# Splitting the ring's loads by partition between two issuing engines

## The chip, the cores and the metric

The kernel runs on one core of a Trainium2 chip. The metric is the device time of one execution in microseconds (us). The kernel before takes 869.49 us, the median of three runs (869.4 to 870.17). One execution of it was profiled; that one took 869.43 us, of which the profile's span covers 867.6 us.

The engines are named as in the profile: PE is the matrix engine, PEld its weight loads, DVE the vector engine, ACT the scalar engine (ScalarE), POOL GpSimd and SP the sync engine (SyncE). SP does nothing here but issue transfers. Each engine works through its own instructions in the order in which they were written; an instruction that waits holds up everything behind it on that engine.

## The reference

The kernel computes two layers of a decoder for one token of 8 sequences, all in float32. Each layer is an attention block with a cache of keys and values, and a dense block with GELU. Both layers use the same weights and the same caches:

```python
def _A_ref(x, k_cache, v_cache, wq, wo):          # x 8x1x1024, caches 8x4x4096x128
    q = (x @ wq).reshape(B, Sq, Hq, Dh)           # 32 query heads, 4 heads of keys
    scores = einsum("bhqd,bhkd->bhqk", q, k) * (Dh ** -0.5)
    p = softmax(scores)
    o = einsum("bhqk,bhkd->bhqd", p, v)
    return o.reshape(B, Sq, Hq * Dh) @ wo
def _B_ref(x, w1, b1, w2, b2):                    # 1024 -> 3584 -> 1024
    h = gelu(einsum("bsd,df->bsf", x, w1) + b1)
    return einsum("bsf,fd->bsd", h, w2) + b2
x = x + _A_ref(_layernorm(x), ...)
x = x + _B_ref(_layernorm(x), ...)
x = x + _A_ref(_layernorm(x), ...)
x = x + _B_ref(_layernorm(x), ...)
```

## The kernel before, in words

Nearly all of its time goes into reading weights and caches from device memory: with 8 rows of activations each loaded element is used for little arithmetic. All loads go into one large tile of on-chip memory, `arena`, 128 partitions by 218 units of 256 floats (1 KB per partition and unit). Three areas of 64 units, A, Bb and C, take loads of 8 MB (128 partitions of 64 KB each): one sequence's keys or values for all four heads, or half of `wq` or `wo`. A fourth area is the **ring**: four slots R[0] to R[3] of 8 units, which take loads of 1 MB (128 partitions of 8 KB each).

The order of the loads is a list, `stream`, that is written out at build time: for layer 0 `wq`, then keys and values of sequences 0 to 7, then through the ring `wo` ("o0", 16 loads), `w1` ("i0", 14 loads), `w2` ("p0", 13 loads of 1 MB and two of 0.5 MB) and `wq` again ("q1", 14 loads of 1 MB, one of 0.75 MB and one of 0.5 MB). After that layer 1 goes through the caches from the last sequence to the first, in large loads again, and its `wo`, `w1` and `w2` come in large loads too. While the ring runs, the areas A, Bb and C still hold caches of the last sequences, which layer 1 uses without loading them again.

`take` marks units as used and `give` as free. `give` is called behind the matmuls that read a load last, and it calls `pump`, which issues every load at the head of `stream` whose units are free (L183 to L191). Everything is recorded in the order of the program; the issuing instruction then waits on the chip until those matmuls are done. In the kernel before, all loads of `stream` are issued by SP (L190), so SP's order is the order of `stream`.

In the ring, `expand` (L200, matmuls at L217) and `project` (L307, matmuls at L314) read one load after another; each load takes PE some eight or sixteen matmuls, then its slot is given back and the load four places further on is issued into it. Between them stand the layer norms (`layernorm`, L146: a Square at L167 and a Sqrt at L174 on ACT) and the GELU (`hidden_unit`, L280: a Tanh at L291 on ACT between DVE operations).

Of the kernel before, what the change touches and what calls it, by code (L numbers as in the profile page):

```python
# [14 lines left out]
P = 128  # L15
# [37 lines left out]
def decode_layers(ctx: ExitStack, tc: tile.TileContext, x, kc, vc, wq, wo, w1, w2, w2_low, out):  # L53


    nc = tc.nc
# [12 lines left out]
    def is_free(at, n):  # L69
        return not any(u in used for u in range(at, at + n))  # L70

    def take(at, n, who):
        assert is_free(at, n), (who, at, n)
        used.update(dict.fromkeys(range(at, at + n), who))

    def give(at, n):
        for u in range(at, at + n):
            used.pop(u)
        pump()
# [99 lines left out]

    stream = []  # L180
    held = {}

    def pump():  # L183
        while stream and is_free(stream[0][1], stream[0][2]):
            key, at, n, src = stream.pop(0)
            take(at, n, key)
            dst = arena[:, at * KB:at * KB + src.shape[1]]
            if key[0] == "low":
                dst = arena[key[1]:LOW:4, AT_LOW * KB:AT_LOW * KB + src.shape[1]]
            nc.sync.dma_start(out=dst, in_=src)  # L190
            held[key] = at, n  # L191

    def loads(name):
# [403 lines left out]
    open_queries()  # L597
    rsum = row_sums()
    pump()
    nc.vector.tensor_reduce(rsum, x_row, AX.X, ALU.add)  # L600

# [162 lines left out]
```

## Time and profile before

| | |
|---|---|
| median of 3 runs | 869.49 us |
| the profiled execution | 869.43 us, its span 867.6 us |
| PE busy / DVE busy / ACT busy | 541.9 / 175.3 / 52.9 us |
| moved from device memory | 368.47 MB, 425 GB/s over the span |
| stretch with 8 MB loads, 60 to 340 us | 432 GB/s |
| stretch of the ring, 345 to 505 us | 419 GB/s |
| stretch with large loads, 565 to 830 us | 432 GB/s |

The profile's page gives busy time per engine, then the span in 40 slices of 21.7 us each. The line DMA there is the mean busy share of the core's 16 DMA engines, in tenths; GB/s is what they moved. A DMA queue holds the transfers of one issuing engine; each transfer is cut into packets over the 16 DMA engines. The chain of waits follows the work that ended last back to the start, at each step to what released it. The answers on stretches of time give, for each stretch, its length, the busy time and count of PE, PEld, DVE, ACT and POOL, then the granted clock of PE, the busy share of the DMA engines (1.00 is all of them, all the time) and GB/s.

### The profile page before, as it was taken

The page shows a single profiled execution, that of the slowest core. Times are in us where ns is not written, and L with a number is a line of the kernel's source. Part 1 is how long each engine was busy: PE and PEld are TensorE (multiplying, and loading weights), DVE is VectorE, ACT ScalarE, POOL GpSimd, SP SyncE. Part 2 cuts the span into 40 slices and gives each one's busy share as a digit, 9 for nine tenths or more (in the row PEclk, how much of TensorE's full clock was granted, in tenths as well). Part 3 has the DMA queues.
Part 4 walks back from the last instruction along what each step waited for, and adds up shares of the span by engine and source line. Part 5 has one row for each costly group of instructions (what it writes and reads, how often), then busy time and mean ns, then how long its engine had stood idle before and what let it go on. Part 6 is the DMA issues. An engine that isn't in the chain of part 4 may idle for free.

```text
span 867.6 us, 8713 instructions
## 1 busy us (share of the span) xinstructions
PE 541.9 (62%) x3896; PEld 173.1 (20%) x3896; DVE 175.3 (20%) x458; ACT 52.9 (6%) x84; POOL 3.5 (0%) x14
## 2 busy tenths in 40 slices
PE   0556575655656566867676587776574654665677
PEld 0112121211212122221221132222121211211222
DVE  0001231313122232200110023332231313120011
ACT  0200000000000011000000010000000000000100
POOL 0000000000000000000000000000000000000000
PEclk9977787777777877766876888977787777777789
DMA  9999999999999999999999999999999999999997
GB/s 393 436 436 433 435 430 433 435 433 433 435 430 433 435 417 426 407 419 421 420 420 420 421 420 437 438 433 433 435 433 433 435 433 435 433 432 433 420 425 308
DMA packets 16669, 369.06 MB, mean 425 GB/s; under 512 B 1868, under 2 KB 2028, under 8 KB 2924
## 3 DMA queue, kind: packets, MB, share of 16 engines
q1 hardware_dynamic: 16488, 368.36, 99.3%
q8 instruction: 30, 0.49, 0.2%
q10 hardware_dynamic: 144, 0.15, 0.0%
q14 instruction: 7, 0.06, 0.0%
HBM read 368.47 MB, written 0.03 MB: 425 GB/s over the span
## 4 chain that ended last, share of the span: by engine, by line
DMA 77%; PE 20%; DVE 1%; ACT 1%; issue 0%; SPq 0%; POOL 0%; ACTq 0%; POOLq 0%
DMA arena<-in_A_k_cache_dram 22%; DMA arena<-in_A_v_cache_dram 21%; DMA arena<-in_B_w_dram 16%; DMA arena<-in_A_wo_dram 10%; DMA arena<-in_A_wq_dram 8%; PE sps L483 6%; PE sps L426 6%; PE sps L217 2%; PE sps L314 2%; PE sps L497 1%; PE spot L339 1%; PE sps L461 0%; ACT arena L450 0%; DVE arena L434 0%; ACT arena L464 0%
## 5 line engine op out<-in xcount | busy, mean ns | idle before, releaser
L426 PE MATMUL sps<-arena 128*32 128x512 f32 x992 | 142.4, 712 | 116.6 <-DMA arena<-in_A_k_cache_dram 104.4
L483 PE MATMUL sps<-arena 128*32 128x512 f32 x1024 | 151.7, 732 | 19.6 <-DMA arena<-in_A_v_cache_dram 19.6
L217 PE MATMUL sps<-arena,xnT 128*32 128x512 f32 (+3 forms) x592 | 77.0, 650 | 37.3 <-DMA arena<-in_A_wq_dram 19.3
L426 PEld LDWEIGHTS sps<-arena 128*32 128x32 f32 x992 | 31.2, 124 | 192.6 <-DMA arena<-in_A_k_cache_dram 96.8
L314 PE MATMUL sps<-arena,oT 128*32 128x256 f32 x496 | 50.5, 546 | 22.4 <-DMA arena<-in_B_w_dram 10.6
L490 DVE TENSOR_TENSOR sps<-sps,misc 128x512 f32<-128x512 f32 x64 | 44.3, 692 | 65.0 <-PE sps L483 65.0
L461 PE MATMUL sps<-ident,arena 128*128 128x128 f32 x128 | 28.8, 365 | 43.5 <-ACT arena L450 31.6
L483 PEld LDWEIGHTS sps<-arena 128*32 128x32 f32 x1024 | 33.0, 130 | 95.6 <-issue 72.5
L450 ACT ACTIVATE arena<-arena,bias 128x1024 f32<-128x1024 f32 x16 | 18.4, 1147 | 492.2 <-DVE scratch L447 492.2
L434 DVE TENSOR_SCALAR_CACHE_REDUCE arena<-sps 128x512 f32<-128x512 f32 x32 | 22.1, 691 | 124.6 <-PE sps L426 124.6
L491 DVE TENSOR_REDUCE scratch<-sps 128x128 f32<-128x512 f32 x64 | 44.2, 691 | 2.2
L499 DVE TENSOR_TENSOR oT<-sps,scratch 128x8 f32<-128x8 f32 x64 | 11.0, 172 | 160.5 <-PE sps L497 160.5
L217 PEld LDWEIGHTS sps<-arena,xnT 128*32 128x32 f32 x592 | 18.1, 127 | 84.3 <-DMA arena<-in_A_wq_dram 30.3
L497 PEld LDWEIGHTS sps<-misc,scratch 128*128 128x128 f32 x128 | 21.5, 211 | 66.0 <-DVE scratch L491 39.9
L339 PE MATMUL spot<-arena,oT 128*32 128x512 f32 x120 | 16.9, 717 | 18.9 <-DMA arena<-in_A_wo_dram 18.9
L461 PEld LDWEIGHTS sps<-ident,arena 128*128 128x128 f32 x128 | 18.2, 179 | 51.8 <-ACT arena L450 35.5
L497 PE MATMUL sps<-misc,scratch 128*128 128x8 f32 x128 | 27.4, 286 | 1.2 <-DVE scratch L491 1.2
L314 PEld LDWEIGHTS sps<-arena,oT 128*32 128x32 f32 x496 | 17.1, 142 | 53.3 <-DMA arena<-in_A_wo_dram 19.6
L339 PE MATMUL spot<-arena 128*32 128x512 f32 (+2 forms) x108 | 17.9, 682 | 1.8 <-DMA arena<-in_B_w_dram 1.8
L466 DVE COPY arena<-sps 128x512 f32<-128x512 f32 x16 | 11.1, 691 | 37.1 <-PE sps L461 37.1
L156 PE MATMUL sps<-nmean,rsum 128*128 128x64 f32 x8 | 2.0, 336 | 25.3 <-DVE rsum L600 23.7
L468 PE MATMUL sps<-scratch,misc 128*128 128x32 f32 x32 | 10.0, 404 | 12.5 <-DVE arena L466 12.5
(105 smaller groups left out, 163.2 us busy)
## 6 DMA issues: line engine op xcount, KB each, us to landing
arena<-in_B_w_dram SPq DMA_DIRECT2D x27, 1024.0 KB, 8.0
arena<-in_A_wo_dram SPq DMA_DIRECT2D x16, 1024.0 KB, 8.7
arena<-in_A_wq_dram SPq DMA_DIRECT2D x14, 1024.0 KB, 8.7
arena<-in_A_k_cache_dram SPq DMA_DIRECT2D x3, 4096.0 KB, 17.8
arena<-in_A_v_cache_dram SPq DMA_DIRECT2D x3, 4096.0 KB
arena<-in_A_v_cache_dram SPq DMA_DIRECT2D x4, 2048.0 KB, 11.2
arena<-in_B_w_dram SPq DMA_DIRECT2D x1, 6144.0 KB, 45.9
arena<-in_B_w_dram SPq DMA_DIRECT2D x1, 5120.0 KB, 39.4
```

Of the source, the lines that this page charges most:

```text
L217: nc.tensor.matmul(acc[32 * j:32 * j + 32, r * P:(r + len(ts)) * P], xnT[:, kt * B:kt * B + 32], blocks[:, ts[0] - t0:ts[-1] - t0 + 1:4], ...
L314: nc.tensor.matmul(y[32 * j:32 * j + 32, a:a + n], weights, data, start=(j not in begun), stop=stop)
L339: nc.tensor.matmul(y2[32 * j:32 * j + 32, h * CH:(h + 1) * CH], weights, data, start=((h, j) not in begun2), stop=stop)
L426: nc.tensor.matmul(ps[32 * g:32 * g + 32, :], q[:, c:c + 32], kt[:, g * CH:(g + 1) * CH], start=(j == 0), stop=(j == HKV - 1))
L434: nc.vector.tensor_scalar(row[:, half * CH:(half + 1) * CH], ps, SCALE, None, op0=ALU.mult, op1=ALU.max, accum_out=st["mx"][:, half:half + 1])
L450: nc.scalar.activation(row, row, AF.Exp, bias=bias, scale=1.0, accum_out=ls)
L461: nc.tensor.transpose(pp[:, t * P:(t + 1) * P], row[:, c:c + P], ident)
L466: nc.vector.tensor_copy(s[:, half], src)
L483: nc.tensor.matmul(o[32 * g:32 * g + 32, :], s[:, g], v[:, g * CH:(g + 1) * CH], start=(half == 0), stop=(half == NH - 1))
L490: nc.vector.tensor_tensor(blocks, blocks, sel_t.unsqueeze(2).to_broadcast([P, T, DH]), ALU.mult)
L491: nc.vector.tensor_reduce(r, o.rearrange("p (t d) -> p d t", t=T), AX.X, ALU.add)
L497: nc.tensor.matmul(po[:, 0:REP], scratch[:, a:a + DH], sel_h, start=True, stop=True)
```

## The change

Each load of "o0", "i0", "p0" and "q1" that covers at least 6 units (0.75 or 1 MB) is made as two loads. SP issues partitions 0 to 63, ACT issues partitions 64 to 127. That concerns 58 loads (16 + 14 + 13 + 15). The three loads of 0.5 MB in the ring, all large loads and everything on the compute engines stay as they are. The matmuls that read such a load wait for both halves.

```diff
+    HALVED_LOADS = ('o0', ('i0', 0), ('i0', 1), 'p0', ('q1', 0), ('q1', 1))
 
     def pump():
         while stream and is_free(stream[0][1], stream[0][2]):
...
-            nc.sync.dma_start(out=dst, in_=src)
+            if key[0] in HALVED_LOADS and n >= 6:
+                nc.sync.dma_start(out=dst[0:P // 2], in_=src[0:P // 2])
+                nc.scalar.dma_start(out=dst[P // 2:P], in_=src[P // 2:P])
+            else:
+                nc.sync.dma_start(out=dst, in_=src)
             held[key] = at, n
```

In the changed kernel the two new issuing lines are L192 (SP) and L193 (ACT), the old one is L195, and the lines behind them move down by 5.

On SP nothing moves; the rows of the ring's loads are half as high. This is SP's list from the last loads of layer 0's values to the first of layer 1's, in the kernel before:

```order
L190 DMA arena<-in_A_v_cache_dram 128x2048 x2
L190 DMA arena<-in_A_wo_dram 128x2048 x16
L190 DMA arena<-in_B_w_dram 128x2048 x27
L190 DMA arena<-in_B_w_dram 128x1024 x2
L190 DMA arena<-in_A_wq_dram 128x2048 x11
L190 DMA arena<-in_A_wq_dram 128x1536
L190 DMA arena<-in_A_wq_dram 128x2048 x3
L190 DMA arena<-in_A_wq_dram 128x1024
L190 DMA arena<-in_A_v_cache_dram 128x4096 x2
```

and with the change (`B_w` is `w1` and then `w2`):

```order
L195 DMA arena<-in_A_v_cache_dram 128x2048 x2
L192 DMA arena<-in_A_wo_dram 64x2048 x16
L192 DMA arena<-in_B_w_dram 64x2048 x27
L195 DMA arena<-in_B_w_dram 128x1024 x2
L192 DMA arena<-in_A_wq_dram 64x2048 x11
L192 DMA arena<-in_A_wq_dram 64x1536
L192 DMA arena<-in_A_wq_dram 64x2048 x3
L195 DMA arena<-in_A_wq_dram 128x1024
L195 DMA arena<-in_A_v_cache_dram 128x4096 x2
```

The places and the order are the same; 58 rows have 64 partitions in place of 128.

On ACT, which issued only the load of `x` before, the other halves now stand between its own instructions. This is the piece of the difference on ACT over layer 0's second layer norm (Square L167, Sqrt L174) and its two GELUs (Tanh, L296):

```order
+L193 DMA arena<-in_A_wo_dram 64x2048 x13
+L193 DMA arena<-in_B_w_dram 64x2048 x4
+L167 ACTIVATE scratch,ss<-x_all,nmu 128x256
+L193 DMA arena<-in_B_w_dram 64x2048 x2
+L174 ACT_TABLE_LOAD
+L174 ACTIVATE sd<-sps,misc 128x1
+L193 DMA arena<-in_B_w_dram 64x2048 x7
+L296 ACT_TABLE_LOAD
+L296 ACTIVATE scratch<-scratch 128x128
+L193 DMA arena<-in_B_w_dram 64x2048 x7
+L296 ACTIVATE scratch<-scratch 128x96
+L193 DMA arena<-in_B_w_dram 64x2048 x7
```

A half that stands behind a Square, a Sqrt or a Tanh is issued only after it, and those three stand behind the halves ahead of them, each of which waits until the matmuls have left its slot.

## The prediction

> **What bounds the kernel now.** I read the page's slices first, then its chain of waits:
>
> ```profile
> DMA  9999999999999999999999999999999999999997
> GB/s 393 436 436 433 435 430 433 435 433 433 435 430 433 435 417 426 407 419 421 420 420 420 421 420 437 438 433 433 435 433 433 435 433 435 433 432 433 420 425 308
> ...
> DMA 77%; PE 20%; DVE 1%; ACT 1%; issue 0%; SPq 0%; POOL 0%; ACTq 0%; POOLq 0%
> ```
>
> The DMA engines are busy in every slice and carry 77% of the chain: the kernel takes as long as its bytes take. But the rate is not the same throughout. From slice 15 to slice 24, where the ring runs, it is about 420 GB/s, elsewhere 433 to 436. The stretches say it more sharply (third column from the right: granted clock; then DMA share, GB/s):
>
> ```profile
> 60.00:340.00 280.00, 170.90 (x1094) 53.03 (x1094) 67.69 (x168) 13.79 (x22) 0.00 (x0) 0.77 1.00 432
> 345.00:505.00 160.00, 112.50 (x961) 35.24 (x965) 17.31 (x50) 8.95 (x15) 0.16 (x1) 0.73 1.01 419
> ```
>
> Both have a DMA share of 1.00 or 1.01: in the ring too, no DMA engine is idle. So the ring is not short of transfers in flight; its bytes only cost more engine time each. The DMA view of the same two stretches says why (queue 1 is SP's; packets, MB, share of 16 engines):
>
> ```profile
> q1 hardware_dynamic: 2421, 120.78, 99.9%
> ...
> q1 hardware_dynamic: 9251, 66.88, 101.0%
> ```
>
> Take the engine time as so much per MB and so much per packet. Stretch one: 280 us x 16 x 0.999 = 4476 engine-us for 120.78 MB and 2421 packets. Stretch two: 160 x 16 x 1.010 = 2586 for 66.88 MB and 9251 packets. The two equations give 36.8 engine-us per MB (435 GB/s over 16 engines) and 0.0136 us per packet. The ring's rate is lower because its rows are 8 KB, not 64 KB, and each is a packet. The change keeps the rows at 8 KB.
>
> How much lies ahead of a load when it is issued:
>
> ```profile
> arena<-in_B_w_dram SPq DMA_DIRECT2D x27, 1024.0 KB, 8.0
> ...
> 403.73 8.77 DMA arena<-in_B_w_dram
> 412.50 0.04 issue
> 412.55 1.11 PE sps L217 x8
> 413.67 8.77 DMA arena<-in_B_w_dram
> ```
>
> In the chain, a slot goes round in 413.67 - 403.73 = 9.94 us, during which four loads land, so one load takes 2.49 us. From issue to landing a load needs 8.0 us at the median, of which 8.0 - 2.5 = 5.5 us are spent behind earlier loads. That is the cover: a transfer issued 1 us later lands no later, while the queues are not dry.
>
> **The change part by part.** *Bytes and rows*: the same, nothing.
>
> *Completions*: each load's packets include one small one per DMA engine, which reports it done. 58 loads more, 16 engines each, are 928 packets; at 0.0136 us over 16 engines this is 928 x 0.0136 / 16 = **+0.8 us**. It lies on the DMA engines, which set the end, so all of it counts. Bounds: nothing, if the second queue's data fills the gap; 1.6 us at double price.
>
> *Two queues in place of one*: the ring's two halves now alternate on every DMA engine. The trace has one case, the load of `x` on ACT's queue beside the first 8 MB load on SP's:
>
> ```profile
> x_all<-in_A_x_dram ACTq DMA_DIRECT2D x1, 146.0 KB, 22.4
> ```
>
> 146 KB should take under half a microsecond at 435 GB/s; it takes 22.4 us because its few rows per engine wait their turn between rows of 64 KB. In just that time, slice 1 of the page, the rate is 393 of 436, a loss of 21.7 x (1 - 393/436) = 2.1 us, which includes the start of everything. So taking turns between the queues costs next to nothing there. But that load covers all 128 partitions, as nearly all others do. The nearest loads with fewer are the four of 3 partitions each near the end, and their data is too little to give a rate. What happens when each queue aims at one half of the partitions, the trace does not show. From below, I bound it by what a perfect overlap of the packets' gaps could give: the 58 loads hold 57.75 x 1.0486 = 60.6 MB, 144.5 us at 419 GB/s and 140.2 us at 432, so **-4.3 us**. From above, by the halves taking turns entirely, each at half the rate, 216 GB/s: 280.4 us, **+136 us**. I take 0 for the forecast, being nearest to the one row with two queues, and keep both ends.
>
> [...]
>
> *Issuing*: SP's transfers and those that are not full height stand in one view of line 190:
>
> ```profile
> L190 SPq DMA_DIRECT2D arena<-in_A_wo_dram x18: 327/328/431, 326.2 to 748.9; - x18
> L190 SPq DMA_DIRECT2D arena<-in_low_dram x4: 642/664/837, 786.3 to 789.0; - x4
> ```
>
> A full load takes SP 0.33 us to issue, one of 3 partitions 0.64 to 0.84 us. A half lies between them in height; I take 0.33 to 0.84 us, so at most 0.5 us later than now. On SP as on ACT there is one per 2.49 us, and 0.5 us is a tenth of the cover of 5.5 us: **0 us**. Without cover, 58 x 0.5 = 29 us.
>
> *What waits on ACT*: the halves there stand behind a Square, a table load with Sqrt, or a table load with Tanh, and hold those up in turn. ACT has room, 8.95 us busy of the ring's 160. The tightest place is the GELU:
>
> ```profile
> 422.13 1.28 ACT L291 ACT_TABLE_LOAD   x1 [19.99 <-DVE scratch L290]
> 423.43 0.31 ACT L291 ACTIVATE scratch<-scratch 128x128 f32<-128x128 f32 x1
> ...
> 422.48 1.07 PE L217 MATMUL sps<-arena,xnT 128*32 128x128 f32 x16 [0.21 <-DMA arena<-in_B_w_dram]
> ```
>
> The next half behind this Tanh becomes free when PE leaves that load, at 422.48 + 1.07 = 423.55; Tanh ends at 423.74. The half is 0.2 us late, covered. The Sqrt of the layer norm waits in turn for a half ahead of it, whose slot PE leaves one load later than now, so its table load of 1.28 us falls up to 2.5 us later. Behind it DVE takes the reciprocal, which is first used at the end of the unit, eight loads on: covered too. Price without cover: about 1.5 us at each of the four places, 6 us.
>
> *Late halves at the turns*: the program has eight counters for landed transfers, in turn. Before, eight loads could be under way; now it is eight halves, four loads, which is just the ring. At the first loads of i0 and q1 the turn is out of step and SP's half waits until ACT's half of two loads earlier has landed. Six loads are concerned. Then one load, 2.49 us, is still ahead of it, against 0.33 to 0.84 us of issue and the way to the memory. I take 0.1 us for each, **+0.6 us**, between 0 and, if each loses half a load's time, 7 us.
>
> Sum: 0.8 + 0.6 = +1.4 us on the profiled execution's 869.43 (span 867.6 and 1.8 around it): **870.9 us**, 0.06 us more when set against the median of 869.49. The end of the ring doesn't swallow it: behind it DMA stays busy (slices 24 and 25 above), so what comes late there ends late.
>
> **The rivals.** *The halves hinder each other.* If the DMA engines that carry a half together can only reach part of the write side at a time, each row takes longer, and each 1% on the row adds 1.45 us, since the ring has no slack. For it: a half covers half the partitions, and in a full load each engine's rows may go to partitions of its own. Against it: alternating rows give both halves work at every moment. It would take anything from 2% more, 872 us, past a row a third longer, 918 us, to taking turns, 869.5 + 136 = 1005 us. It decides from a row that is 2% longer than now.
>
> *The gaps close.* If two queues let one half's next row be fetched during the other's gap, the ring runs at the 432 GB/s of large rows and saves 4.3 us: 865.2 us. For it: the fitted 0.0136 us per packet. Against it: the share of 101.0% says that packets already overlap a little.
>
> *The cover fails.* ACT and SP issue different halves at different times and a load counts only when the later one is there. If issue at 0.84 us, the waits on ACT and the counters together exceed the 5.5 us, each load loses up to 0.5 us: 29 us, 898 us. Against it: the rows of ACT above.
>
> **How the numbers follow.** About 0.2%, 1.7 us, is what a measurement of this kernel can tell from no change. Forecast, no hindrance: 0.42, its own range 869 to 873; of this 0.27 lies within 0.2% and 0.15 above. Hindrance: 0.33, spread evenly from 872 to 1005. Closed gaps: 0.17. Failed cover: 0.08. So faster 0.17, same 0.27, slower 0.15 + 0.33 + 0.08 = 0.56. The range leaves out the upper part of the hindrance, beyond 955 (0.33 x 50/133 = 0.12), and the last of the closed gaps below 866 (0.05): 866 to 955 us.
>
> **What would show it.** In the changed profile, the stretch of the ring should still show a DMA share of 1.00 and close to 419 GB/s, with as many bytes on ACT's queue as on SP's, about 30 MB each. A share near 1.00 at a much lower rate, with time from issue to landing well above 8 us, would be hindrance. A share clearly below 1.00 would be failed cover, with SP or ACT named as releaser. About 430 GB/s would be closed gaps. The stretches of large loads must not change; if they do, my account of the ring is wrong.

## The result and the profile after

With the change the kernel takes 970.51 us, the median of four runs (967.6 to 979.51), against 869.44 us before: 1.118 times as long, 95% interval 1.114 to 1.121, 101 us more. The forecast was 870.9 us and the range 866 to 955; both missed. That both say slower is no merit of the forecast: its +1.4 us came from other terms, and the loss is one that it put at 0 and kept as a rival, halves that hinder each other. Where two runs of one kernel lie more than 1.5% apart, as below with 951.6 and 999.2 us, only the faster one is compared.

The page's slices of the changed kernel (a slice is 24.4 us now), its queues (queue 1 SP's, queue 10 ACT's: packets, MB, share of 16 engines), and the stretches with 8 MB loads, of the ring, and with large loads again (last columns: granted clock, DMA share, GB/s):

```profile
DMA  9999999999999999999999999999999999999997
GB/s 392 446 413 467 425 427 432 427 430 442 430 430 426 380 311 211 252 245 227 259 265 267 249 249 247 428 429 449 430 432 427 430 437 438 438 427 432 426 422 308
...
q1 hardware_dynamic: 12776, 338.08, 86.8%
q10 hardware_dynamic: 4784, 30.43, 12.7%
...
60.00:340.00 280.00, 170.20 (x1081) 52.88 (x1085) 66.86 (x164) 13.79 (x22) 0.00 (x0) 0.77 1.00 427
345.00:605.00 260.00, 132.14 (x918) 41.03 (x921) 16.27 (x50) 9.54 (x17) 0.16 (x1) 0.55 1.01 250
680.00:940.00 260.00, 156.13 (x1019) 47.55 (x1009) 56.31 (x140) 13.38 (x22) 1.17 (x1) 0.77 1.00 431
```

The large loads run as before: from 60 to 310 us at 433 GB/s against 434, and the 427 in place of 432 up to 340 us comes from the end, where ACT's first half is already loading. The ring runs at 250 GB/s in place of 419. The profiled execution is the slowest of the four, and its span is 977.6 - 867.6 = 110 us longer than that of the kernel before. The 60.6 MB of halved loads take 60.6 / 0.250 = 242 us in place of 144.5, 98 of these 110 us; with the other loads of the stretch, 65.0 MB in all, it is 260 us in place of 155, 105 of the 110. The DMA share is still 1.01: no DMA engine is idle, the same rows only take longer. The bytes are the same, 368.5 MB in all.

The chain of waits in the ring, and the page's issues of the halves:

```profile
397.91 14.63 DMA arena<-in_A_wo_dram
412.55 0.04 issue
412.59 1.98 PE sps L319 x16
414.59 14.78 DMA arena<-in_A_wo_dram
...
arena<-in_B_w_dram ACTq DMA_DIRECT2D x27, 512.0 KB, 12.4
arena<-in_A_wo_dram SPq DMA_DIRECT2D x16, 512.0 KB, 12.4
```

A slot goes round in 414.59 - 397.91 = 16.7 us where it took 9.9, and the halves shown take 12.4 us from issue to landing where a whole load took 8.0 to 8.7.

### The profile page after: what moved, and what is told of

Same layout as the page of the kernel before. It is cut to its first block, busy times and chain, and to the rows that moved or that the text cites. A ratio compares the mean times of both kernels' runs of the same rounds, so it can differ in the third digit from the quotient of the medians.

```text
span 977.6 us, 8889 instructions
## 1 busy us (share of the span) xinstructions
PE 570.5 (58%) x3896; PEld 180.4 (18%) x3896; DVE 175.6 (18%) x458; ACT 52.9 (5%) x84; POOL 3.5 (0%) x14
## 2 busy tenths in 40 slices
DMA packets 17598, 369.07 MB, mean 378 GB/s; under 512 B 2796, under 2 KB 2956, under 8 KB 3852
## 4 chain that ended last, share of the span: by engine, by line
DMA 81%; PE 17%; DVE 1%; ACT 1%; issue 0%; SPq 0%; ACTq 0%
DMA arena<-in_A_v_cache_dram 24%; DMA arena<-in_A_k_cache_dram 19%; DMA arena<-in_B_w_dram 17%; DMA arena<-in_A_wo_dram 10%; DMA arena<-in_A_wq_dram 10%; PE sps L488 5%; PE sps L431 5%; PE sps L222 2%; PE sps L319 2%; PE spot L344 1%; PE sps L502 1%; PE sps L466 0%; DVE arena L439 0%; ACT arena L455 0%; DVE scratch L496 0%
## 5 line engine op out<-in xcount | busy, mean ns | idle before, releaser
L431 PE MATMUL sps<-arena 128*32 128x512 f32 x992 | 145.2, 724 | 119.4 <-DMA arena<-in_A_k_cache_dram 107.3
L488 PE MATMUL sps<-arena 128*32 128x512 f32 x1024 | 154.4, 743 | 29.1 <-DMA arena<-in_A_v_cache_dram 29.1
L222 PE MATMUL sps<-arena,xnT 128*32 128x512 f32 (+3 forms) x592 | 88.5, 731 | 67.1 <-DMA arena<-in_B_w_dram 37.2
L319 PE MATMUL sps<-arena,oT 128*32 128x256 f32 x496 | 56.5, 600 | 63.3 <-DMA arena<-in_A_wo_dram 31.4
L319 PEld LDWEIGHTS sps<-arena,oT 128*32 128x32 f32 x496 | 19.8, 152 | 98.0 <-issue 69.1
L344 PE MATMUL spot<-arena,oT 128*32 128x512 f32 x120 | 17.9, 756 | 17.6 <-DMA arena<-in_A_wo_dram 17.6
L247 DVE TENSOR_SCALAR scratch<-sps,rs 128x512 f32<-128x512 f32 (+1 forms) x8 | 5.7, 718 | 83.8 <-PE sps L222 83.8
## 6 DMA issues: line engine op xcount, KB each, us to landing
arena<-in_B_w_dram ACTq DMA_DIRECT2D x27, 512.0 KB, 12.4
arena<-in_A_wo_dram SPq DMA_DIRECT2D x16, 512.0 KB, 12.4
```

The source lines that it names most:

```text
L222: nc.tensor.matmul(acc[32 * j:32 * j + 32, r * P:(r + len(ts)) * P], xnT[:, kt * B:kt * B + 32], blocks[:, ts[0] - t0:ts[-1] - t0 + 1:4], ...
L319: nc.tensor.matmul(y[32 * j:32 * j + 32, a:a + n], weights, data, start=(j not in begun), stop=stop)
L344: nc.tensor.matmul(y2[32 * j:32 * j + 32, h * CH:(h + 1) * CH], weights, data, start=((h, j) not in begun2), stop=stop)
L431: nc.tensor.matmul(ps[32 * g:32 * g + 32, :], q[:, c:c + 32], kt[:, g * CH:(g + 1) * CH], start=(j == 0), stop=(j == HKV - 1))
L488: nc.tensor.matmul(o[32 * g:32 * g + 32, :], s[:, g], v[:, g * CH:(g + 1) * CH], start=(half == 0), stop=(half == NH - 1))
```

## The experiments

Five theories were set against each other. A: which partitions a load covers decides how fast its rows land. B: two queues taking turns cost the time. C: a load of 64 rows is slow by itself. D and E, later, are about why two halves together don't make up for it: D, that pairs of DMA engines work on the same half at the same moment; E, that the loss comes with every such half, whatever the engines' turns. All kernels differ from the changed one only in the lines that issue the halves. The kernel before took 869.6 to 870.2 us as the median beside each set of runs.

### Both halves from one queue

```diff
-                nc.scalar.dma_start(out=dst[P // 2:P], in_=src[P // 2:P])
+                nc.sync.dma_start(out=dst[P // 2:P], in_=src[P // 2:P])
```

> Both halves of each of the 58 loads issued by SyncE, one behind the other; ScalarE issues none. Theory A (the DMA engines that carry one half share their way into the half's partitions, whatever queue it came from): as slow as the change or slower, ring at 217 to 250 GB/s, 960 to 1005 us. Theory B (two queues taking turns row by row is what costs): back to about 871 us, ring at 415 to 419 GB/s. Theory C (a row of a load of 64 partitions is slower by itself, for instance by the way its packets are made): about 970 us as the change.

The run that is compared took 951.6 us, 82 us more than before; a second took 999.2 us. The stretch of the ring in the faster one:

```profile
345.00:580.00 235.00, 130.09 (x922) 41.53 (x921) 16.93 (x50) 8.95 (x15) 0.16 (x1) 0.55 1.02 278
```

Slow with one queue too. 278 GB/s is above the 217 to 250 that A had expected, and 951.6 us below its 960, so the size was missed; but it is far from B's 415 to 419 GB/s. The second queue is not what makes the change slow; B falls. A and C stand.

### Split by columns

```diff
+                half = src.shape[1] // 2
+                nc.sync.dma_start(out=dst[:, 0:half], in_=src[:, 0:half])
+                nc.scalar.dma_start(out=dst[:, half:], in_=src[:, half:])
```

> The 58 loads split by columns in place of partitions: each half covers all 128 partitions with rows of 4 KB, one from SyncE, one from ScalarE. Theories A and C: no hindrance, but 58 x (128 + 16) more packets at 0.0136 us over 16 engines, +7 us: about 877 us, ring near 400 GB/s. Theory B: two queues take turns as in the change, over still more rows: 970 us or more.

876.89 us (ratio 1.008, 1.006 to 1.010), 7.3 us more, where 7 were worked out from the packets. The ring:

```profile
345.00:510.00 165.00, 114.77 (x965) 34.45 (x965) 17.39 (x50) 10.42 (x18) 0.16 (x1) 0.73 1.02 403
```

Two loads per slot from two engines, the same bytes, twice the packets, and next to no hindrance. What hurts is how the change cuts the load, not that it is cut. (The agreement on the microsecond is partly luck: a pair of runs further down shows that a second queue has a price of its own, which was not in the 7 us.)

### Even and odd partitions

```diff
+                nc.sync.dma_start(out=dst[0:P:2], in_=src[0:P:2])
+                nc.scalar.dma_start(out=dst[1:P:2], in_=src[1:P:2])
```

> The halves of the change, but SyncE takes the even partitions and ScalarE the odd ones, so each half spans the whole height of the memory. If the change is slow because 64 neighbouring partitions are only one half of the memory's height (A in its simplest form): hindrance gone, about 871 us, ring near 415 GB/s. If it is slow because the rows are dealt out in order over the 16 engines, so that pairs of engines meet at the same place in any half (A as pairs): slow again, 230 to 260 GB/s, 950 to 990 us. Theory C: about 970 us. Theory B: about 970 us.

884.98 us (two runs, 885.0 and 884.95), neither 871 nor 970. The stretches, and the wait that stands out, show two things at once:

```profile
356.00:360.00 4.00, 1.11 (x4) 0.71 (x4) 0.28 (x1) 1.62 (x3) 0.00 (x0) 0.50 0.04 14
368.00:372.00 4.00, 2.59 (x24) 1.01 (x20) 2.81 (x6) 0.59 (x1) 0.00 (x0) 1.00 0.09 12
376.00:520.00 144.00, 91.25 (x871) 30.68 (x864) 11.29 (x39) 8.36 (x14) 0.84 (x2) 0.77 1.01 412
...
ACT arena L469 <- DMA arena<-in_A_wo_dram: 15.7, 1, 15.7
```

From 376 us on, the ring runs at 412 GB/s: halves of 64 rows, two queues, no hindrance. C falls, since these rows are as many and as long as in the change. Before that the DMA engines stand almost idle in two gaps: at the end of the attention an ACT copy into `arena` (L469, L464 in the kernel before) waits 15.7 us for the ring's first load. No other kernel's trace has this wait; in the kernel before, the same copy waits 1.3 us for PE. A likely reason, not tested by itself, is that the rows of the strided half are taken to overlap the copy's target. So the run was made again without that.

### The same, with the ring's first four loads whole

```diff
+                if key in [('o0', i) for i in range(4)]:
+                    nc.sync.dma_start(out=dst, in_=src)
+                else:
+                    nc.sync.dma_start(out=dst[0:P:2], in_=src[0:P:2])
+                    nc.scalar.dma_start(out=dst[1:P:2], in_=src[1:P:2])
```

> Even partitions from SyncE and odd ones from ScalarE, as in the run before, but the ring's first four loads whole, so that no instruction at the end of the attention waits for a half. If the 15 us of that run over the kernel before are the stall at its first load and not the halves: 870 to 873 us, ring at 412 to 419 GB/s. If the halves cost it: about 884 us.

876.2 us (ratio 1.008, 1.006 to 1.009). The stall was 8.8 of the 15 us; 6.5 us remain, a miss of 3 us against the expected 870 to 873. The ring has 405 GB/s at a DMA share of 1.00, below the expected 412 to 419 too:

```profile
345.00:510.00 165.00, 111.31 (x993) 38.07 (x993) 17.51 (x52) 8.95 (x15) 0.84 (x2) 0.74 1.00 405
```

### One half alone: the lower, the middle, the even

Here the disputed cost stands alone: the ring's first four loads whole, then only one half of each load, all from SP. The other half is left out, so the matmuls read old data there. These are the lines of three kernels, one each:

```diff
+                    nc.sync.dma_start(out=dst[0:P // 2], in_=src[0:P // 2])   # the lower
+                    nc.sync.dma_start(out=dst[32:96], in_=src[32:96])         # the middle
+                    nc.sync.dma_start(out=dst[0:P:2], in_=src[0:P:2])         # the even
```

> The disputed cost by itself: the ring's first four loads whole, of the other 54 only partitions 0 to 63, all from SyncE; the upper halves are not loaded at all, so the ring moves about half its bytes and the matmuls read old data there. Theory A (64 neighbouring partitions from 0 on are reached over half of the write side): a half takes almost as long as a whole load did, ring at about 217 to 250 GB/s with a DMA share near 1.00, 54 x 0.524 MB at 217 GB/s = 130 us where 134 us stood before: about 865 us, 850 at 250 GB/s. Rival (both halves in flight together is what hinders): rows as fast as before, the ring limited by the matmuls, DMA share well below 1.00, 800 to 840 us.

> As the run with the lower half only, but with partitions 32 to 95 in its place: 64 neighbours too, the same bytes, the same issuing. [...] If any 64 neighbours, or any load of 64 rows, is slow: the same time as the lower half, 850 to 865 us.

> As the run with the lower half only, but with the 64 even partitions: the same bytes and rows. Theory A (the whole height is reached): rows as fast as in a whole load, ring limited by the matmuls, DMA share well below 1.00, 800 to 840 us, as with the middle half. If a load of 64 rows is slow by its packets: 850 to 865 us as the lower half.

The lower half: 875.1 us (874.4 and 875.8). The middle half: 832.4 us (831.2 and 833.5). The even half: 829.4 us (826.6 and 832.1). The last two lie in the 800 to 840 us that theory A gave for both. The ring of each, in this order:

```profile
385.00:505.00 120.00, 79.35 (x687) 24.79 (x687) 9.22 (x35) 7.97 (x14) 0.16 (x1) 0.74 1.01 209
```

```profile
385.00:465.00 80.00, 58.62 (x651) 20.96 (x647) 10.38 (x36) 8.36 (x14) 0.42 (x2) 0.90 0.85 294
```

```profile
385.00:465.00 80.00, 59.20 (x647) 23.23 (x643) 10.71 (x38) 8.36 (x14) 0.88 (x2) 0.89 0.86 297
```

This is the clearest pair of the study. Partitions 0 to 63 and partitions 32 to 95 are both 64 neighbours, with the same bytes and the same issuing. The lower half keeps the DMA engines fully busy at 209 GB/s, just half of 419: half the bytes take as long as all of them, and the kernel is 5 us slower than before although it loads 28 MB less. With the middle half the DMA engines have 15% of their time to spare at 294 GB/s, and the kernel ends 37 us earlier. So neither the number of rows nor their being neighbours counts, but which 64 of the 128 they are. Why 0 to 63 are slower than 32 to 95, no run shows.

Three limits of this pair. What holds the middle half back is not shown: the expectation that names both halves has the matmuls as the limit, but PE is busy for 58.6 of the 80 us and still waits 17.9 us for loads. Nor are its rows shown to be as fast as a whole load's: for a share of 1.00 the lines give, as an estimate, 294 / 0.85 = 346 GB/s, against 419 / 1.01 = 415 for whole loads and 209 / 1.01 = 207 for the lower half. The even half alone gives 345 too, though even and odd halves together, further down, go at 416, so this gap may come from having one half alone in flight. And rows 0 to 63 of `arena` are also rows 0 to 63 of the weights, so no run parts the place written from the place read. In the kernel's layout the rows lie 128 KB apart in `wo` and `wq` and 112 KB apart in `w1` and `w2`; the lower half is slow in both (204 GB/s from 400 to 450 us with `w1` and `w2`, 207 from 470 to 500 us with `wq`), which speaks against the place read but is no test of it.

The lower half's expected 850 to 865 us was missed by its lower rate, 209 against the 217 to 250 GB/s used there.

### Whole loads in turn from two engines

```diff
+                issuer = (nc.sync, nc.scalar)[len(ringed) % 2]
+                ringed.append(key)
+                issuer.dma_start(out=dst, in_=src)
```

> The 58 loads stay whole, 128 partitions and rows of 8 KB; every other one is issued by ScalarE. Theories A and C: no hindrance, 865 to 871 us (865 if two queues close the gaps between packets, 869.5 if not). Theory B: as slow as the change, about 970 us.

883.77 us (ratio 1.014, 1.011 to 1.017): missed by every theory. The ring:

```profile
345.00:520.00 175.00, 106.09 (x922) 36.09 (x925) 16.24 (x49) 8.56 (x15) 0.16 (x1) 0.70 0.96 372
```

It is another loss than the change's: the DMA share falls to 0.96, so here the DMA engines do run short. One reading, argued from the share and not shown, is that two whole loads in two queues land close together, and that their slots come free late because PE uses them one after the other. ACT's own work between the loads can have a part in it too.

### Whole loads, all from ACT; even and odd, both from SP

```diff
+                nc.scalar.dma_start(out=dst, in_=src)                             # whole, ACT
+                    nc.sync.dma_start(out=dst[0:P:2], in_=src[0:P:2])             # even and odd, SP,
+                    nc.sync.dma_start(out=dst[1:P:2], in_=src[1:P:2])             # first four whole
```

> Open: why whole loads issued in turn by SyncE and ScalarE took 14 us more than before. All 58 loads whole and all issued by ScalarE, so that the ring is one queue again. If two queues taking turns row by row is the cause (two loads then land together and the ring runs short): gone, 869 to 873 us, ring at 415 to 420 GB/s. If issuing behind ScalarE's own work is the cause: 880 us or more, with ScalarE's line as releaser.

> Open: what the 6.5 us are that even and odd halves from two queues cost over the kernel before. The same halves, first four loads of the ring whole, but both issued by SyncE, one behind the other. If the second queue is the cost: 869 to 872 us. If it is the halves (58 more loads, their packets and their issue): 874 to 878 us.

Whole loads from ACT: 879.58 us (ratio 1.011, 1.009 to 1.013). That is the 880 us of the second theory, but most of it not at its place. Stretches of the ring, one of them narrow, and ACT's issues:

```profile
345.00:385.00 40.00, 26.26 (x214) 9.80 (x216) 7.00 (x14) 2.21 (x4) 0.00 (x0) 0.71 0.82 332
385.00:425.00 40.00, 28.60 (x214) 7.08 (x213) 0.98 (x5) 2.14 (x4) 0.00 (x0) 0.63 1.01 417
425.00:465.00 40.00, 23.51 (x283) 9.70 (x279) 6.21 (x22) 1.87 (x3) 0.16 (x1) 0.86 1.01 421
465.00:510.00 45.00, 31.55 (x234) 9.14 (x238) 2.84 (x9) 4.34 (x7) 0.00 (x0) 0.67 0.99 401
...
360.00:365.00 5.00, 2.16 (x13) 0.46 (x10) 0.00 (x0) 0.00 (x0) 0.00 (x0) 0.63 0.11 44
...
314.86 0.33 ACTq L192 DMA_DIRECT2D arena<-in_A_wo_dram  x1
347.40 0.82 ACTq L192 DMA_DIRECT2D arena<-in_A_wo_dram  x2
364.92 30.68 ACTq L192 DMA_DIRECT2D arena<-in_A_wo_dram  x13
```

About 8 of the 9.7 us go at the ring's start, where 40 us at 332 GB/s stand in place of 412. The ring's first loads no longer stand behind the last values of the attention in SP's queue; they overtake them (the first at 314.86 us, where SP issued it at 326.2 before). From 360 to 365 us the DMA engines then have almost nothing to move, until ACT issues the next loads from 364.92 us on; that the free slots were full by then is the reading of these times. About 2 us more go from 465 us on, where the kernel before keeps 420 GB/s and this one has 401. The ring's second layer norm stands there on ACT. The even and odd halves from two queues fall to 400 GB/s in the same stretch, and the same halves from SP alone, next, keep 420. So issuing behind ACT's own work is probably not free, though no run takes it by itself.

Even and odd from one queue: 870.5 us over ten runs, ratio 1.0005, interval 0.9996 to 1.0015.

```profile
345.00:510.00 165.00, 110.29 (x1021) 39.26 (x1025) 19.23 (x56) 8.95 (x15) 0.84 (x2) 0.78 1.01 416
```

So 54 halved loads cost 0.7 us, not clear of zero, when the halves span the whole height and come from one queue. Issuing one half from ACT costs the other 5.8 of the 6.5 us, about 2 of them in the stretch of the second layer norm; how much the queue itself takes is not separated.

### Shifting the engines' turns

What stays: two halves in flight cover all 128 partitions between them, and still get only 250 to 280 of 419 GB/s. Theory D was that pairs of DMA engines work on the same half at the same moment. On the kernel with both halves from SP, the fifth load's lower half was cut into smaller loads, meant to give eight of the engines four, or as a control eight, rows more than the others. This is the cut for four rows; for eight, the lower half is made of eight loads of 8 rows:

```diff
+                if key == ('o0', 4):
+                    for j in range(4):
+                        nc.sync.dma_start(out=dst[j:32:4], in_=src[j:32:4])
+                    nc.sync.dma_start(out=dst[32:64], in_=src[32:64])
+                else:
+                    nc.sync.dma_start(out=dst[0:P // 2], in_=src[0:P // 2])
+                nc.sync.dma_start(out=dst[P // 2:P], in_=src[P // 2:P])
```

> Open after the runs so far: two halves in flight together could use the whole write side between them, and reach only 250 to 280 GB/s. Theory D (pairs of DMA engines run in step: both work on the lower half's rows at the same moment, then both on the upper's). As the run with both halves in SyncE's queue, 951 to 999 us, where each engine has four rows of the lower half and then four of the upper; but the fifth load of the ring is cut so that eight of the engines get four rows more than the other eight: partitions 0 to 31 in four loads of 8 rows, 32 to 63 in one, then the upper half. Nothing else moves. Theory D: the pairs are then half a turn apart, and from there on the ring runs well above 300 GB/s, 870 to 910 us. Theory E (the loss comes with every half whatever the engines' turns): 950 to 1000 us.

> Control for the shift: the fifth load's lower half in eight loads of 8 rows, so that eight of the engines get eight rows more, a full turn of four and four. Theory D: back in step, as slow as without a shift, 940 to 1000 us. Theory E: the same, 950 to 1000 us. If it is fast as the run with four rows, the shift helps in another way than D says.

993.56 us (986 to 996) with four rows and 1001.63 us (1000 to 1003) with eight. The stretch from 400 to 600 us, with four and with eight:

```profile
400.00:600.00 200.00, 91.95 (x647) 28.98 (x651) 8.98 (x33) 6.75 (x12) 0.16 (x1) 0.52 1.02 234
```

```profile
400.00:600.00 200.00, 89.33 (x635) 28.34 (x635) 8.23 (x32) 6.17 (x11) 0.16 (x1) 0.52 1.02 225
```

The shift brought nothing; D falls in the form in which it was tested. Both kernels are slower than the 951.6 us of the one without a shift, and 1001.63 us is just beyond E's 1000; why is open. That form of D rests on which rows go to which DMA engine. The pages count 2828 and 2844 packets under 512 B, 32 and 48 more than the 2796 of the kernel without a shift: that is 8 for each load of 8 rows, where every other half has 16. But the trace doesn't name the engine of a packet, so running in step by another dealing of the rows isn't excluded. Why the two halves together reach 250 GB/s, more than one half's 209 and far less than 419, stays open.

## Why the prediction was wrong

**What bounds the kernel** held. The ring is bound by engine time per row at a DMA share of 1.01, and what it loses the kernel loses: its stretch accounts for 105 of the 110 us between the two profiled executions.

**The completions**, +0.8 us, fit: the page of the changed kernel counts 2796 packets under 512 B against 1868, the 928 more that the term counts, and even and odd halves from one queue cost 0.7 us (interval -0.3 to 1.3), with 54 of the 58 loads halved. A cost of zero fits as well. The split by columns came out at the 7 us that the price of 0.0136 us per packet gives, but it has a second queue too, so it doesn't confirm that price.

**"Two queues in place of one"** is the step that failed. It took 0, "being nearest to the one row with two queues", between bounds of -4.3 and +136 us. The value is about +98 us. The row that it leaned on, the load of `x` beside the first 8 MB load, covers all 128 partitions; it spoke to the turns of two queues and was silent on the partitions. The prediction said so itself ("what happens when each queue aims at one half of the partitions, the trace does not show"), and yet the nearest row was allowed to decide. Two things were rolled into one term there. The partitions: from one queue the split at partition 64 costs 82 us (951.6 us), and 123 and 131 us in the two kernels that cut one load differently (993.56 and 1001.63). The second engine: with halves that span the height it costs 5.8 us, not 0.

**The rival that halves hinder each other** was the right one, with 0.33. Its argument against itself, "alternating rows give both halves work at every moment", is what the runs refute: from 360 to 600 us SP's queue took 53.5% of the engines' time and ACT's 47.4%, so both halves were at hand throughout, and the rate was 247 GB/s. Its point of decision, rows 2% longer, was passed by far: 419 / 250 is 68% longer. Its upper end, the halves taking turns entirely, was 1005 us; 970.5 was measured, and 250 GB/s is 20% above one half's 209. That the halves together keep every engine busy doesn't explain the loss: the even and odd halves do so too (a share of 1.01) and lost 0.05% from one queue.

**Issuing** was bounded at 0.33 to 0.84 us and is 0.47 us on SP and 0.50 us on ACT:

```profile
L192 SPq DMA_DIRECT2D arena<-in_A_wo_dram x16: 465/466/600, 334.7 to 418.8; - x16
L193 ACTq DMA_DIRECT2D arena<-in_A_wo_dram x16: 488/497/554, 314.8 to 418.8; - x16
```

Even and odd halves from one queue, where SP issues both, lose 0.7 us in all, so it is covered, as forecast.

**What waits on ACT** was put at 0 and followed through the ring's layer norm and GELU. Where loads come from ACT without the hindrance, the stretch of the second layer norm loses about 2 us, so 0 was probably too low there. The place that cost more was not looked at: the ring's start, where a load on ACT's queue overtakes those that wait in SP's. Alone, with whole loads, that costs about 8 us; in the change both are hidden in the rest. The late halves at the turns (+0.6 us) can't be told apart from that.

**The other rivals.** The gaps between packets didn't close: no run with two queues reached 419 GB/s. The cover didn't fail in the change, whose DMA share stays at 1.01; with whole loads in turn the engines did run short, at 0.96.

**The range** left out the hindrance beyond 955 us as 0.12 of the chance. That cut went through a rival whose price was open over 130 us, with nothing in the trace to say where in it the value lies.

## What to carry to other kernels

A load that is split by partitions is not two halves of the same thing: split by columns, or by even and odd partitions, it kept its rate within 4%, split at partition 64 it fell to 60%. When the only argument for a price of zero is a row that doesn't contain the new feature, the price is unknown. And a second issuing engine isn't free even where it does no harm to the rows: it cost 5.8 us on 54 loads, and with whole loads it let the ring's first one, issued at 314.86 us in place of 326.2, overtake the last values of the attention.

## What the runs showed of the hardware

- 64 partitions from 0 on load at 209 GB/s with every DMA engine busy; 64 partitions from 32 on go at 294 GB/s with the engines 85% busy, the 64 even ones at 297 with 86%. A whole load's rows go at 419.
- Lower and upper halves in one stream have no steady rate. Within the 951.6 us run from one queue it went from 262 GB/s (345 to 420 us) to 279 (420 to 500 us) and 294 (500 to 580 us); with a single load cut differently it was 234 and 225 GB/s (400 to 600 us).
- A load of 64 neighbouring partitions takes 0.47 us to issue on SP and 0.50 us on ACT, where one of 128 takes 0.33 us on SP.
